# Attention, gated feed-forward and token mixing: the probabilities' fp16 parts taken straight from the exponentials, and the last attention unit's scores taken from fp32 products

## The chip, the cores and the metric

The program runs on one core of a Trainium2 chip. The engines are TensorE (PE, whose weight loads are listed apart as PEld), VectorE (DVE), ScalarE (ACT), GpSimd (POOL) and SyncE (SP), which issues every DMA here. The metric is the device time of one execution in microseconds, as the median of several runs.

## The reference

Three layers follow one another. Only the first is touched by the change.

```python
# B, H, S, D = 2, 8, 768, 64; n_sink 4, window 128
scores = (1 / sqrt(D)) * q @ k.T
keep = (key < n_sink) | ((0 <= query - key) & (query - key < window))
a = softmax(where(keep, scores, -1e9))      # row sum plus 1e-9
x = (a @ v) as (B, S, 512)

h = relu(x @ w_in)                          # 512 -> 1024
x = (h * sigmoid(conv3(h))) @ w_out         # back to 512; conv3 along the sequence

theta = x @ w_theta
y = w_tok_r @ (x * cos(theta)) + w_tok_i @ (x * sin(theta))
u = x + y
out = u + relu(u @ w_ch)
```

Everything is fp32. The weights arrive as 64-bit words and are decoded on the chip by ACT and DVE.

## The kernel before

**Products in parts.** Most products are made of three matmuls on a high part (fp32r) and a low part (the rest) of each side: `hi*hi + hi*lo + lo*hi`. The high part is a copy by ACT, the low part a subtraction by DVE. `split`, `decode` and `mm3` are the helpers.

**Attention** runs in four units of eight heads: batch 0 first half of the queries (unit 0), batch 0 second half (unit 1), then batch 1 likewise (units 2 and 3). A unit is four pairs of heads. Because of the window, a tile of 128 queries needs only its own block of keys, the block before, and the four sink keys: 260 columns, except the very first tile of a sequence, which needs 128. `head` does one head:

1. `scores`: one product for each of three query tiles. In units 0 to 2 it is one fp32 matmul against a buffer `qk` that holds both heads of a pair (L299). In unit 3 it is a "stack": `load_stack` loads q and k of one head twice, one copy below the other, ACT and DVE make fp32r parts of them (L82, L283 on ACT, L84, L284 on DVE), and two fp32r matmuls give the product (L296). The first stack head is prepared ahead, after unit 2's last pair; the schedule puts that at about 98 us.
2. DVE adds the mask and takes the row maximum (L315); ACT takes the exponential with the row sum (L319); DVE makes the reciprocal `ri` (L322, L323).
3. For 28 of the 32 heads (`NORM` is `ACT`) the probabilities then go to fp16 parts: ACT multiplies the three tiles by `ri` in place (L335), ACT casts to the high part `hi` (L345), DVE subtracts to the low part `lo` (L346), and POOL makes the parts of the sink columns (L349, L350). All lie in a buffer `pb`. SP transposes it by DMA into `pt` (L353). In the four heads of unit 0's first two pairs PE does the transpose instead.
4. `pair_out` multiplies `pt` by the values (L411), and ACT and DVE write the parts of the next layer's input `xg` (L431, L432).

A head of a first half (units 0 and 2) casts in two pieces, 128 and 512 columns; a head of a second half (units 1 and 3) in one of 768.

**The second layer** is interleaved: `Group.blocks` does a block of two 128-wide slices of the hidden layer for 256 tokens (24 matmuls into `ps_h`, 12 into `ps_x`, and ACT and DVE work between them: `h`, `cv`, `ghi`, `glo`). `BLOCKS` puts blocks behind pairs of heads, and `CHUNKS` puts the decoding of its weights behind pairs of units 0 and 1. A block needs `xg` of its tokens, hence the attention before it. The rest of the second layer and the third layer follow after unit 3.

**The order** on each engine is fixed when the program is built: a list scheduler with its own model of time places the instructions of all these loops, so a shorter step moves others. Each engine then runs its list in order. PSUM has two buffers for scores, `e` three, `pb` three, `pt` four.

Of the kernel before, what the change touches and what calls it, by code (L numbers as in the profile page):

```python
# [263 lines left out]
def stack_buffer(pool, n):  # L264
    return [pool.tile([P, w], F32R, name=f"stack{n}{i}") for i, w in enumerate((3 * P, 4 * KW, 4 * KW))]


def load_stack(tc, c, n):


    nc = tc.nc
    unit, h = divmod(n, H)
    b, half = divmod(unit, 2)
    k0, nk = (0, 3 * KW - NS) if half == 0 else (2 * KW, 4 * KW - NS)
    raw = c.stack_raw[n % 2]
    q, k1, k2 = c.stack[n % 2]
    rows = slice(h * D, (h + 1) * D)
    qr, kr = raw[:, : 3 * P], raw[:, 3 * P : 3 * P + nk]
# [712 lines left out]
```

## Time and profile before

| | |
|---|---|
| Runs | 475.7, 479.04, 496.11 us; median 479.04 |
| Profiled execution | 475.81 us, of which the span is 474.0 us |
| Unit 1 (last exponentials of units 0 and 1) | about 51 to 109 us |
| Unit 2, unit 3 | about 109 to 155 us, 155 to 203 us |
| Rest of the second layer on PE | to about 296 us |
| Third layer | to the end, 474 us |

The windows below are cut at the ends of the units. "Busy" counts the union of an engine's instructions; an instruction's duration overlaps the start of the next, so the price of one in a row of them is read from start to start. The granted clock is a share of TensorE's 2.4 GHz; its two levels are 1.2 and 2.4 GHz, so 0.93 means that about 14% of the time was at the lower one.

### The profile page before, as it was taken

The page shows a single profiled execution, that of the slowest core. Times are in us where ns is not written, and L with a number is a line of the kernel's source. Part 1 is how long each engine was busy: PE and PEld are TensorE (multiplying, and loading weights), DVE is VectorE, ACT ScalarE, POOL GpSimd, SP SyncE. Part 2 cuts the span into 40 slices and gives each one's busy share as a digit, 9 for nine tenths or more (in the row PEclk, how much of TensorE's full clock was granted, in tenths as well). Part 3 has the DMA queues.
Part 4 walks back from the last instruction along what each step waited for, and adds up shares of the span by engine and source line. Part 5 has one row for each costly group of instructions (what it writes and reads, how often), then busy time and mean ns, then how long its engine had stood idle before and what let it go on. Part 6 is the DMA issues. An engine that isn't in the chain of part 4 may idle for free.

```text
span 474.0 us, 7252 instructions
## 1 busy us (share of the span) xinstructions
PE 418.8 (88%) x2376; PEld 341.0 (72%) x2376; DVE 337.1 (71%) x870; ACT 316.2 (67%) x773; POOL 23.2 (5%) x92
## 2 busy tenths in 40 slices
PE   2877648797699899799999999899889999999994
PEld 1665336685488778688898888588668888888873
DVE  5689979997578997875699877897389973211132
ACT  2999869999999999985686877966475431100010
POOL 4101001010100101100000000000000000000000
PEclk9997778899979989899999999999989999999998
DMA  4888998567984665360434100131016730000012
GB/s 109 250 198 201 281 256 206 130 168 143 189 145 86 148 139 113 73 99 12 152 114 121 60 0 1 45 90 44 0 51 197 232 100 22 24 22 24 22 44 75
DMA packets 74589, 51.94 MB, mean 110 GB/s; under 512 B 59696, under 2 KB 63280, under 8 KB 74544
## 3 DMA queue, kind: packets, MB, share of 16 engines
q1 hardware_dynamic: 74544, 51.40, 43.6%
q8 instruction: 21, 0.34, 0.3%
q14 instruction: 24, 0.20, 0.1%
HBM read 33.95 MB, written 3.15 MB: 78 GB/s over the span
## 4 chain that ended last, share of the span: by engine, by line
PE 61%; ACT 15%; DVE 10%; DMA 9%; issue 3%; SPq 1%; POOL 0%; DVEq 0%; ACTq 0%
PE ps_y L125 7%; PE ps_y L124 7%; PE ps_y L126 7%; DMA pt<-pb 5%; PE ps_x L651 4%; PE ps_m L126 4%; PE ps_m L125 4%; PE ps_m L124 4%; PE ps_x L652 4%; PE ps_x L657 3%; PE ps_h L124 3%; PE ps_h L126 3%; PE ps_h L125 3%; ACT e L335 3%; ACT e L319 3%
## 5 line engine op out<-in xcount | busy, mean ns | idle before, releaser
L299 PE MATMUL ps_s<-qk 128*128 128x260 f32 (+1 forms) x144 | 48.7, 450 | 19.8 <-POOL sink_rows L221 8.7
L124 PE MATMUL ps_h<-xg_hi,win_hi 128*128 128x258 f32 x192 | 58.5, 306 | 1.8 <-ACT h L632 1.8
L124 PE MATMUL ps_y<-z_hi,wt_hi 128*128 128x512 f32 x144 | 57.6, 400 | 1.3 <-ACT z_hi L82 0.9
L125 PE MATMUL ps_y<-z_hi,wt_lo 128*128 128x512 f32 x144 | 57.0, 397 | 0.1
L126 PE MATMUL ps_y<-z_lo,wt_hi 128*128 128x512 f32 x144 | 56.4, 396 | 0.0
L125 PE MATMUL ps_h<-xg_hi,win_lo 128*128 128x258 f32 x192 | 55.9, 292 | 0.0
L126 PE MATMUL ps_h<-xg_lo,win_hi 128*128 128x258 f32 x192 | 55.7, 296 | 0.0
L82 ACT ACTIVATE xt_hi<-ps_t 128x512 fp32r<-128x512 f32 x24 | 13.9, 595 | 61.4 <-PE ps_t L685 61.4
L315 DVE CUSTOM_DVE_ANT_0 e<-ps_s,m 128x260 f32<-128x260 f32 (+1 forms) x96 | 37.6, 400 | 17.6 <-PE ps_s L299 12.1
L636 DVE SCALAR_TENSOR_TENSOR cv<-h,cw_t,cv 128x256 f32<-128x256 f32 x96 | 44.5, 480 | 7.4 <-ACT cv L634 6.8
L319 ACT ACTIVATE e<-e,mx 128x260 f32<-128x260 f32 (+1 forms) x96 | 47.7, 501 | 1.0 <-DVE mx L315 1.0
L299 PEld LDWEIGHTS ps_s<-qk 128*128 128x128 f32 x144 | 27.3, 226 | 28.9 <-DVE mx L315 12.0
L651 PE MATMUL ps_x<-wout_hi,ghi 128*128 128x512 f32 x96 | 41.3, 430 | 2.5 <-ACT ghi L82 2.5
L124 PEld LDWEIGHTS ps_h<-xg_hi,win_hi 128*128 128x128 f32 x192 | 38.2, 199 | 4.7 <-ACT h L632 2.6
L652 PE MATMUL ps_x<-wout_lo,ghi 128*128 128x512 f32 x96 | 40.1, 417 | 0.0
L753 DVE SCALAR_TENSOR_TENSOR slot<-ps_m,slot 128x512 f32<-128x512 f32 x12 | 8.3, 691 | 44.2 <-PE ps_m L126 44.2
L125 PEld LDWEIGHTS ps_h<-xg_hi,win_lo 128*128 128x128 f32 x192 | 38.2, 199 | 1.3
L126 PEld LDWEIGHTS ps_h<-xg_lo,win_hi 128*128 128x128 f32 x192 | 37.6, 198 | 0.9
L411 PE MATMUL ps_o<-pt,vp 128*64 128x256 f16 (+2 forms) x348 | 25.4, 268 | 13.7 <-DMA pt<-pb 11.7
L335 ACT ACTIVATE e<-e,ri 128x260 f32<-128x260 f32 (+1 forms) x84 | 36.1, 508 | 0.0
L411 PEld LDWEIGHTS <-vp 128*64 128x64 f16 (+1 forms) x348 | 18.8, 116 | 23.5 <-issue 14.9
L124 PEld LDWEIGHTS ps_y<-z_hi,wt_hi 128*128 128x128 f32 x144 | 27.1, 188 | 8.0 <-ACT z_hi L82 1.2
(146 smaller groups left out, 984.6 us busy)
## 6 DMA issues: line engine op xcount, KB each, us to landing
raw<-in_w_tok_r_dram SPq DMA_DIRECT2D x12, 384.0 KB, 3.2
raw<-in_w_tok_i_dram SPq DMA_DIRECT2D x12, 384.0 KB, 3.2
...
```

The lines of the kernel that those rows point to most:

```text
L124: nc.tensor.matmul(out, whi, xhi, start=first, stop=False)
L125: nc.tensor.matmul(out, wlo, xhi, start=False, stop=False)
L126: nc.tensor.matmul(out, whi, xlo, start=False, stop=last)
L299: nc.tensor.matmul(ps[:, :n], qk[0][:, a, i * P : (i + 1) * P], qk[1][:, o : o + n], start=True, stop=True)
L315: nc.vector.tensor_tensor_reduce(out=e[:, i, :n], in0=ps[:, :n], in1=m, scale=-1.0 / math.sqrt(D), scalar=3.0e38, op0=ALU.add, op1=ALU.min ...
L319: nc.scalar.activation(e[:, i, :n], e[:, i, :n], AF.Exp, bias=mx[:, i : i + 1], scale=-1.0, accum_out=sm[:, i : i + 1])
L335: nc.scalar.activation(e[:, i, :n], e[:, i, :n], AF.Copy, scale=ri[:, i : i + 1])
L411: nc.tensor.matmul(po[a * D : (a + 1) * D, q], w[:, a * D : (a + 1) * D], pts[a][: w.shape[0], b0:b1, :], start=(n == 0), stop=(n == len(j ...
L636: nc.vector.scalar_tensor_tensor(cv[:, n, :], h[:, n, k : GT + k], w[:, k : k + 1], cv[:, n, :], ALU.mult, ALU.add)
L651: nc.tensor.matmul(self.px[t], ghi[:, n, s], whi, start=f2 == 0 and n == 0, stop=False)
L652: nc.tensor.matmul(self.px[t], ghi[:, n, s], wlo, start=False, stop=False)
L657: nc.tensor.matmul(self.px[t], glo[:, n, s], whi, start=False, stop=f2 == FB // 2 - 1 and n == 1)
```

## The change

The in-place normalisation is gone. `hi` is now written by ACT from the exponentials with `ri` as scale, once per query tile (three instructions per head), and `lo` by DVE with one `scalar_tensor_tensor` per tile, `e*ri - hi`. POOL makes the normalised sink columns `sk` itself, a third small instruction per head. Unit 3 takes its scores as units 0 to 2 do: `load_stack`, its buffers and its parts are gone, `load_qk` serves all 16 pairs in three rotating buffers, and each tile's score is one fp32 matmul instead of two fp32r ones. The pools that were opened and closed for the stack are gone.

```diff
@@ load_qk @@
-    q, k, _ = c.qk[n % 3 if n < 2 * CC else n % 2]
+    q, k = c.qk[n % 3]
@@ load_stack: removed @@
-    for a in range(2):
-        nc.sync.dma_start(qr[a * D : (a + 1) * D], c.q[b, rows, half * 3 * P : (half + 1) * 3 * P])
-        nc.sync.dma_start(kr[a * D : (a + 1) * D], c.k[b, rows, k0 : k0 + nk])
-    split(nc, k1[:, :nk], k2[:, :nk], kr)
-    nc.scalar.activation(q, qr, AF.Copy)
-    nc.vector.tensor_tensor(q[D:], qr[D:], q[D:].bitcast(F32), ALU.subtract)
@@ scores @@
-    if len(qk) == 3:
-        n = 2 * P + NS
-        for k in qk[1:]:
-            nc.tensor.matmul(ps[:, :n], qk[0][:, i * P : (i + 1) * P], k[:, o : o + n], start=k is qk[1], stop=k is qk[2])
-        return ps
@@ head @@
+    sk = c.st.tile([P, 3, NS], F32, name="sk")[:, s0:, :]
+    nc.gpsimd.tensor_tensor(sk, e[:, s0:, P:KW], ri[:, s0:].unsqueeze(2).to_broadcast([P, ns, NS]), ALU.mult)
     for i in range(3):
-        n = P if half == 0 and i == 0 else 2 * P + NS
-        nc.scalar.activation(e[:, i, :n], e[:, i, :n], AF.Copy, scale=ri[:, i : i + 1])
-    sk = e[:, s0:, P:KW]
-    for i0, i1 in [(0, 3)] if half else [(0, 1), (1, 3)]:
...
-        nc.scalar.activation(hi, src, AF.Copy)
-        nc.vector.tensor_tensor(lo, src, hi, ALU.subtract)
+        first = half == 0 and i == 0
+        d0, d1 = (0, 1) if first else (2 * i - (1 - half), 2 * i + 1 + half)
+        src = e[:, i, :P].unsqueeze(1) if first else two_blocks(e, i, 1)[:, 0]
+        hi, lo, r = pr[:, d0:d1, :], pr[:, nb + d0 : nb + d1, :], ri[:, i : i + 1]
+        nc.scalar.activation(hi, src, AF.Copy, scale=r)
+        nc.vector.scalar_tensor_tensor(lo, src, r, hi, ALU.mult, ALU.subtract)
@@ Unit.pair @@
-            if stack:
-                while len(c.stacked) <= min(2 * n + a + 1, 8 * CC - 1):
-                    c.stacked.append(load_stack(tc, c, len(c.stacked)))
-                qk = c.stacked[2 * n + a]
```

On ACT, at a head of unit 1, the order before (names: `e` exponentials, `ri` reciprocals, `pb` the fp16 parts, `sm` row sums, `mx` row maxima, `dec_t` a weight being decoded, `xg_hi` a part of the next layer's input, `h` a block's hidden slice) is:

```order
L335 ACTIVATE e<-e,ri 128x260 x3
L100 ACTIVATE dec_t<-slot_114 128x512
L431 ACTIVATE xg_hi<-ps_o,vst 128x129
L345 ACTIVATE pb_204<-e 128x768
L319 ACTIVATE e,sm<-e,mx 128x260
L632 ACTIVATE h<-ps_h 128x258
```

And now (L310 is the scaled high part, L288 the exponential, L98 and L80 decoding and parts, L396 the next layer's input):

```order
L310 ACTIVATE pb_199<-e,ri 128x256 x3
L396 ACTIVATE xg_hi<-ps_o,vst 128x257
L98 ACTIVATE dec_t<-slot_119 128x512
L80 ACTIVATE wout_hi<-slot_114 128x512
L288 ACTIVATE e,sm<-e,mx 128x260 x2
L80 ACTIVATE ghi<-cv 128x512
```

The three scaled activations stand where the normalisation stood, write `pb` themselves, and the cast at the end of the head is gone.

On DVE, in unit 1, the low part before (L315 mask and maximum, L346 low part, L101 to L103 decoding):

```order
L101 TENSOR_SCALAR slot_115<-slot_115 128x512
L315 ISA e,mx<-ps_s,m_110 128x260
L315 ISA mx 128x1
L346 TENSOR_TENSOR pb_202<-e,pb_202 128x768
L103 SCALAR_TENSOR_TENSOR slot_119<-slot_119 128x512
L323 RECIPROCAL ri<-sm 128x3
```

And now (L311 is the low part, L284 mask and maximum, L99 to L101 decoding):

```order
L311 SCALAR_TENSOR_TENSOR pb_201<-e,ri,pb_201 128x256 x2
L284 ISA e,mx<-ps_s,m_110 128x260
L284 ISA mx 128x1
L311 SCALAR_TENSOR_TENSOR pb_201<-e,ri,pb_201 128x256
L101 SCALAR_TENSOR_TENSOR slot_118<-slot_118 128x512
L101 SCALAR_TENSOR_TENSOR slot_119<-slot_119 128x512
```

One subtraction over a head became three instructions, which the order splits around other work.

On PE, at the start of unit 3, before (L296 the two matmuls of a stack, L124 to L126 a block's first product, L411 a pair's output):

```order
L411 LDWEIGHTS vp
L411 MATMUL ps_o<-pt,vp 64x256
L126 MATMUL ps_h<-xg_lo,win_hi 128x258
L296 MATMUL ps_s<-stack_1224,stack_1223 128x260
L296 MATMUL ps_s<-stack_1225,stack_1223 128x260
L124 MATMUL ps_h<-xg_hi,win_hi 128x258
L125 MATMUL ps_h<-xg_hi,win_lo 128x258
```

And now (L268 the fp32 score, L122 to L124 the block's first product, L376 the output):

```order
L124 MATMUL ps_h<-xg_lo,win_hi 128x258
L122 MATMUL ps_h<-xg_hi,win_hi 128x258
L123 MATMUL ps_h<-xg_hi,win_lo 128x258
L268 MATMUL ps_s<-qk_120 128x260
L376 LDWEIGHTS vp
L376 MATMUL ps_o<-pt,vp 64x256
```

One fp32 score stands where two fp32r matmuls stood. Counted over the whole order, between the first score of unit 2 and the first score of unit 3 PE had 72 matmuls into `ps_h` and 28 into `ps_x`, and now has 60 and 16; the 12 and 12 stand behind, among unit 3's work. Up to the first score of unit 2 both orders hold the same 108 and 32.

## Rows read from the trace of the kernel before

**Rows 1.** The page: busy time, share of the span and instructions of each engine.

```profile
PE 418.8 (88%) x2376; PEld 341.0 (72%) x2376; DVE 337.1 (71%) x870; ACT 316.2 (67%) x773; POOL 23.2 (5%) x92
```

**Rows 2.** Windows by stage: length, then each engine's busy us, granted clock, DMA share, GB/s.

```profile
40.00:109.00 69.00, 52.01 (x316) 40.55 (x316) 63.72 (x180) 63.36 (x167) 6.44 (x22) 0.80 0.81 198
109.00:155.00 46.00, 38.95 (x281) 31.38 (x281) 32.32 (x121) 44.22 (x131) 4.39 (x20) 0.93 0.77 142
155.00:203.00 48.00, 42.96 (x316) 37.05 (x316) 42.79 (x124) 48.00 (x134) 4.44 (x16) 0.93 0.54 117
203.00:296.00 93.00, 93.00 (x588) 80.64 (x588) 72.20 (x146) 66.76 (x140) 0.41 (x2) 1.00 0.28 71
```

**Rows 3.** Timeline, ACT, two stretches: start us, us, what it ran.

```profile
101.09 0.90 ACT L634 ACTIVATE cv<-h,cw_t 128x256 f32<-128x256 f32 x2
101.89 0.36 ACT L431 ACTIVATE xg_hi<-ps_o,vst 128x129 fp32r<-128x129 f32 x1
...
102.64 1.31 ACT L335 ACTIVATE e<-e,ri 128x260 f32<-128x260 f32 x3
103.85 0.93 ACT L207 ACTIVATE slot<-slot,vst 128x768 f16<-128x768 f32 x1
...
105.69 0.83 ACT L345 ACTIVATE pb<-e 128x768 f16<-128x768 f32 x1
106.43 0.46 ACT L431 ACTIVATE xg_hi<-ps_o,vst 128x257 fp32r<-128x257 f32 x1
...
130.24 0.82 ACT L345 ACTIVATE pb<-e 128x512 f16<-128x512 f32 x2
130.96 1.19 ACT L335 ACTIVATE e<-e,ri 128x128 f32<-128x128 f32 x3
```

**Rows 4.** Timeline, DVE, unit 1.

```profile
103.41 0.88 DVE L636 SCALAR_TENSOR_TENSOR cv<-h,cw_t,cv 128x256 f32<-128x256 f32 x2
104.20 0.35 DVE L432 SCALAR_TENSOR_TENSOR xg_lo<-ps_o,vst,xg_hi 128x129 fp32r<-128x129 f32 x1
...
108.56 0.95 DVE L346 TENSOR_TENSOR pb<-e,pb 128x768 f16<-128x768 f32 x1
109.43 0.48 DVE L432 SCALAR_TENSOR_TENSOR xg_lo<-ps_o,vst,xg_hi 128x257 fp32r<-128x257 f32 x1
```

**Rows 5.** Timeline, ACT, unit 3: parts of one head's k and q.

```profile
188.97 0.69 ACT L82 ACTIVATE stack<-qk 128x524 fp32r<-128x524 f32 x1
...
189.91 0.43 ACT L632 ACTIVATE h<-ps_h 128x258 f32<-128x258 f32 x1
```

**Rows 6.** Timeline, DVE, the same head's parts.

```profile
191.31 0.70 DVE L84 TENSOR_TENSOR stack<-qk,stack 128x524 fp32r<-128x524 f32 x1
...
192.63 0.43 DVE L315 CUSTOM_DVE_ANT_0 e<-ps_s,m 128x260 f32<-128x260 f32 x1
```

**Rows 7.** Timeline, PE, two stretches around one score product each.

```profile
151.15 0.71 PE L299 MATMUL ps_s<-qk 128*128 128x260 f32 x2
151.50 0.47 PE L126 MATMUL ps_h<-xg_lo,win_hi 128*128 128x258 f32 x1
151.81 0.28 PE L124 MATMUL ps_h<-xg_hi,win_hi 128*128 128x258 f32 x1
...
182.47 0.40 PE L296 MATMUL ps_s<-stack,stack 128*128 128x260 f32 x2
182.71 0.28 PE L124 MATMUL ps_h<-xg_hi,win_hi 128*128 128x258 f32 x1
182.83 0.28 PE L125 MATMUL ps_h<-xg_hi,win_lo 128*128 128x258 f32 x1
```

**Rows 8.** The chain of waits, 56 to 72 us: start us, us, what.

```profile
58.43 10.08 DMA pt<-pb
```

**Rows 9.** Tile pb: instructions, duration in ns as min/median/max, first and last start.

```profile
L346 DVE TENSOR_TENSOR pb<-e,pb x40: 280/685/959, 42.5 to 209.6; 128x768 f16<-128x768 f32 x16, 128x128 f16<-128x128 f32 x12, 128x512 f16<-128x512 f32 x12
L349 POOL CAST pb<-e x28: 189/203/767, 37.1 to 206.5; 128x24 f16<-128x24 f32 x16, 128x8 f16<-128x8 f32 x12
```

More of the change, by code (lines that the diff above doesn't have):

```diff
@@ L48 @@
 FLAG = 3
-SK = 'gpsimd'
 WT = 8
-PRE_STACK = 1
 TOK_CUT = 2
@@ L246, in qk_buffer @@
     nc.gpsimd.memset(q[:D, 1, :], 0.0)
-    return q, k, qk
+    return q, k
 def load_qk(tc, c, n):
@@ L261, in load_qk @@
     return q, k
[L264 to L278, printed above, removed]
-    for a in range(2):
-        nc.sync.dma_start(qr[a * D : (a + 1) * D], c.q[b, rows, half * 3 * P : (half + 1) * 3 * P])
-        nc.sync.dma_start(kr[a * D : (a + 1) * D], c.k[b, rows, k0 : k0 + nk])
-    split(nc, k1[:, :nk], k2[:, :nk], kr)
-    nc.scalar.activation(q, qr, AF.Copy)
-    nc.vector.tensor_tensor(q[D:], qr[D:], q[D:].bitcast(F32), ALU.subtract)
-    return q, k1, k2
 def scores(tc, c, half, qk, i, a):
@@ L462, in pair @@
         n = (2 * b + half) * CC + p
-        stack = n >= 3 * CC
-        if not stack:
-            while len(c.loaded) <= (n + AHEAD if n + AHEAD < 2 * CC else min(n + 1, 3 * CC - 1)):
-                c.loaded.append(load_qk(tc, c, len(c.loaded)))
-            qk = c.loaded[n]
+        while len(c.loaded) <= min(n + AHEAD, 4 * CC - 1):
+            c.loaded.append(load_qk(tc, c, len(c.loaded)))
+        qk = c.loaded[n]
         pts = []
         for a in range(2):
-            if stack:
-                while len(c.stacked) <= min(2 * n + a + 1, 8 * CC - 1):
-                    c.stacked.append(load_stack(tc, c, len(c.stacked)))
-                qk = c.stacked[2 * n + a]
             pts.append(head(tc, c, half, a, qk, NORM[n][a]))
-            if n == 3 * CC - 1 and a == PRE_STACK:
-                c.stacked.append(load_stack(tc, c, 3 * H))
             if a == LAG - 1:
@@ L771, in body @@
     c.st = pool(right, "st", 4, "right")
-    early, turn = ExitStack(), ExitStack()
-    right.push(lambda *_: early.close())
     if general:
@@ L791, in body @@
         c.ps_o = pool(right, "ps_o", 2, "right", space=PSUM)
-        c.dec = pool(early, "dec", DEC, "right")
-        c.qk = c.qk[:1] + [qk_buffer(nc, pool(st, "qk", 1, side), n) for n, st, side in ((1, turn, "left"), (2, early, "right"))]
+        c.dec = pool(right, "dec", DEC, "right")
+        pq = pool(right, "qk", 1, "right")
+        c.qk = c.qk[:1] + [qk_buffer(nc, pq, n) for n in (1, 2)]
         c.pbuf = []
@@ L810, in body @@
         unit.start()
-        if n == 2 and not general:
-            early.close()
-            pq = pool(right, "stack0", 1, "right")
-            c.stack_raw = [pq.tile([P, 3 * P + 4 * KW], F32, name="stack_raw"), c.qk0]
-            c.stack = [stack_buffer(pq, 0)]
-            c.stacked = [None] * (3 * H)
-        if n == 3 and not general:
-            turn.close()
-            c.stack.append(stack_buffer(pool(turn, "stack1", 1, "left"), 1))
         for p in range(4):
@@ L834, in body @@
     nc.scalar.activation(c.scratch, c.last_sum, AF.Silu)
-    turn.close()
     right.close()
@@ L921, in moe_stack @@
         c.loaded = [load_qk(tc, c, 0)]
-        c.qk0 = c.qk[0][2]
         c.early = [weight_load(tc, c, n) for n in range(EARLY)]
```

11 lines of the change are left out of this document (2 added, 9 removed).

## Prediction

> **What bounds the kernel now.** I read the page first. PE is busy for 418.8 of 474 us and DVE and ACT for about 70% each [rows 1], so by the averages PE is the bound. The windows by stage say otherwise [rows 2]. From 203 to 296 us PE is busy without a gap: a microsecond of PE work there is a microsecond of time. In unit 3 (155 to 203) ACT is busy for all 48 us and PE for 43. In unit 2 ACT is busy for 44.2 of 46 us while DVE has 13.7 us to spare. In the stretch before, 40 to 109 us, ACT (63.4 of 69) and DVE (63.7) are level, so neither can be relieved alone. After 296 us the third layer is PE's and the change does not touch it. So the question is not how much ACT time the change removes but in which of the stages ACT is what ends last, and what PE, which gets the work in the end, pays.
>
> **Part 1, ACT of the probabilities.** Before, a head of a second half takes three normalisations, 102.64 to 103.85 us, 1.21 us, and one cast, 105.69 to 106.43, 0.74 us. After, three activations with a pointer scale over 256 columns. The block's scaling of 256 columns, the same form, takes 0.80 us for two [rows 3], so three take 1.20: the normalisations turn into the high parts at the same price, and the cast is the saving. For a first-half head the cast's two pieces take 0.72 us (130.24 to 130.96) [rows 3]. That is 16 x 0.74 + 12 x 0.72 = 20.5 us of ACT.
>
> **Part 2, DVE of the probabilities.** One subtraction of 768 columns takes 108.56 to 109.43, 0.87 us. Two scaled subtractions of 256 take 0.79 us [rows 4], three 1.19: 0.32 more for a second-half head, or 0.16 for each instruction more. A first-half head goes from two instructions to three, 0.16 more. Together 16 x 0.32 + 12 x 0.16 = 7.0 us more on DVE.
>
> **Part 3, the stack's parts.** ACT makes one head's two parts in 188.97 to 189.91, 0.94 us [rows 5], DVE in 191.31 to 192.63, 1.32 us [rows 6]. Eight heads: 7.5 us off ACT and 10.6 us off DVE. One of the eight lies at about 98 us, one at the end of unit 2, six in unit 3. Over the whole kernel ACT loses 28.0 us and DVE 3.6 net, but DVE's gain is in unit 3, and its loss in the units before.
>
> **Part 4, PE of unit 3's scores.** This is the part that speaks against the change. The fp32 product at 151.15 delays the matmuls behind it until 151.81, where without it one block matmul (0.12 us, from the two neighbours at 182.71 and 182.83) would have stood: 0.54 us. The stack's two matmuls take 182.47 to 182.71, 0.24 us [rows 7]. So each of the 24 products costs 0.30 us more, 7.2 us in all; the least I can read is to the very next matmul, which starts at 151.50: 0.35 against 0.24 us, 0.11 x 24 = 2.6, if that one's own delay is hidden. I take 6.0, near the upper end, because blocks surround these products in both orders. The Trainium skill (FP8 and Floating Point Precision, TensorE Precision Notes) says that true fp32 makes four passes through the array while reduced fp32 reads a truncated value; two passes more of 260 columns at 2.4 GHz are 0.22 us, an estimate of 5.2 us for the 24, which would make the sum 0.8 us better. The trace shows a product as two records, not four, and a price above that estimate.
>
> **Part 5, POOL and the DMAs.** One more POOL instruction per head of the sort that takes 0.2 us in the median and 0.77 at most [rows 9]. Three of these end before ACT's 1.2 us and DVE's last subtraction, which the transpose waits for too; I cost it at nothing while DVE ends last. The stack's 32 loads become 12 and SP has fewer issues; nothing waits for them in unit 3 now.
>
> **The sum, stage by stage.** It is made against the profiled execution, 475.8 us.
>
> *Up to 109 us.* ACT falls by 9.7 us (four heads at 0.72, eight at 0.74, one stack head). DVE gains 4 x 0.16 + 8 x 0.32 = 3.2 us and gives up 1.3 for the stack head: 65.6 of 69 us. DVE is then the only bound. Its idle time of 5.3 us holds the stall behind one transpose, a DMA of 10.1 us queued behind weight loads [rows 8], which no engine's speed changes. I take -1.0, between -4 (the idle time shrinks, since ACT feeds DVE's decoding sooner) and +2 (DVE's increase lies on the path).
>
> *Unit 2.* ACT falls from 44.2 by 8 x 0.72 and one stack head, 6.7 us, to 37.5. The order also moves 12 matmuls into `ps_h` and 12 into `ps_x` behind it; by 0.40 us for 256 columns ACT's share of these is about 2 us, so 35.5. At the same fill (44.2 of 46, 96%) the unit takes 37.0 us: -9.0. With nothing of the moved work counted it is 39.1, -7; if DMA latency shows up, -5; -11 if the fill rises.
>
> *Unit 3 and the rest to 296 us.* PE decides here: without its gaps unit 3 now holds more PE work than ACT or DVE work. Four terms. The moved matmuls: 12 x 0.12, and 12 of twice the columns at 0.24, +4.3. The fp32 products, +6.0. The gaps that go: 48.0 - 43.0, -5.0. The lower clock that goes with them: a granted 0.93 over 48 us at 90% busy costs 0.07 x 48 x 0.9, -3.0. I leave 2.0 us of new gaps, since PE runs its list in order and waits for a transpose now and then: +4.3, between -1 (fp32 at 2.6, no new gap) and +6.5 (7.2, and 3 us of gaps).
>
> *After 296 us.* 0, with 1.5 either way for a changed order of the third layer's first rotations.
>
> -1.0 - 9.0 + 4.3 = -5.7: **470 us**. So about four fifths of the 28 us taken from ACT bring nothing: the first stage has DVE beside ACT, and the last has PE.
>
> **Rivals.**
>
> *The first stage opens too.* The transposes start earlier since the cast is gone, PE has its outputs sooner, and DVE's decoding is fed without waits: -4, with unit 2 at -11 and the last stage at +1 (fp32 at 4.7, no new gap): -14, **462 us**. For it: ACT is 10.0 of 10 in long pieces there. Against: DVE at 63.7 of 69 has to fit 1.9 us more.
>
> *PE pays everything back.* Unit 2 gains 6, the fp32 products cost 7.2 and PE waits in order for another 3 us: -6 + 6.5 = about 0, **476 us**. For it: any PE time after 155 us counts whole. Against: the lower clock and the gaps of unit 3 are seen, and ACT's 11.6 us less there (8 x 0.74 and 6 x 0.94) removes their cause.
>
> *VectorE takes ACT's place, and the result is slower.* The low part now reads e and hi through DVE for three instructions a head, and POOL reads e once more. The Trainium skill (SBUF, Who interferes with whom) says that a DVE instruction with two SBUF inputs and a GpSimd instruction that reads SBUF hold off each other, whichever comes second. As a mechanism of this kernel: each of the 20 heads of units 0 to 2 loses a POOL instruction's 0.2 us on DVE, 4.0 us, with DVE's own 3.2 less 1.3, and unit 2 gains nothing, while PE's fp32 products stay unpaid by half (+2): **484 us**. It decides once DVE's spare 13.7 us in unit 2 lie where they can't be used. Against it: the 768-column subtraction never took over 959 ns, though POOL's cast beside it ranged from 189 to 767 [rows 9]: POOL gives way, not DVE.
>
> **How the numbers follow.** The forecast 470 has 0.55, the open first stage 0.24, the full payback 0.16, the slower one 0.05. The first three lie between 461 and 477; the executions shown differ among themselves by 3 us without the outlier at 496, so the range is 461 to 478. It leaves out the slower case and tails, 0.2 together. A measurement of this kernel tells about 2% from no change, 9.5 us. Faster by more than that: nearly all of the first rival and a sixth of the forecast, 0.33. Slower by over 2%: most of the slower case, 0.04. Within 2%: 0.63.
>
> **What would show it.** ACT's busy time falls by about 28 us and DVE's by about 4. In the stage up to 109 us the end of unit 1 hardly moves and DVE is above 94% of it. Unit 2 takes 35 to 40 us with ACT still above 93%. In unit 3 PE is above 95% busy at a granted clock near 1, ACT clearly below, and each score there delays its neighbours by about 0.5 us. The prediction is wrong if unit 1 ends more than 4 us earlier, if unit 2 stays above 42 us, or if PE still shows gaps of over 4 us between 145 and 285 us.

## The result, and the profile after

The changed kernel takes 463.93 us in the median of four runs (463.08 to 466.72), the kernel before 479.95 us in the median of four. The ratio is 0.9705, with a 95% interval of 0.9621 to 0.9789; it leaves out the run of before at 496.11 us, which stands 3% above the other three. The profiled execution takes 463.08 us with a span of 461.2, against 475.81 and 474.0: 12.7 us less, where 5.7 were forecast.

The page after, the line of engines that answers to [rows 1]:

```profile
PE 415.2 (90%) x2376; PEld 336.5 (73%) x2376; DVE 334.1 (72%) x898; ACT 291.9 (63%) x717; POOL 36.1 (8%) x120
```

ACT lost 24.3 us of busy time and DVE 3.0, near the forecast 28 and 4. POOL gained 12.9 us; its 28 more instructions are 9.3 of that, 0.2 us each in the median and 0.89 at most.

Windows cut at the ends of units 1, 2 and 3, at the first token-mixing matmul (`ps_y`, 294.6 us) and at 350 us; the first three answer to the first three of [rows 2]:

```profile
40.00:107.40 67.40, 52.40 (x317) 40.78 (x316) 64.59 (x194) 56.28 (x151) 10.95 (x28) 0.82 0.82 199
107.40:143.10 35.70, 30.41 (x245) 24.66 (x245) 28.43 (x120) 33.33 (x105) 7.48 (x24) 1.00 0.98 174
143.10:207.00 63.90, 62.57 (x444) 51.81 (x444) 49.77 (x152) 49.40 (x136) 8.60 (x29) 1.00 0.40 79
207.00:294.60 87.60, 85.68 (x518) 73.59 (x517) 68.03 (x136) 63.44 (x133) 0.62 (x3) 1.00 0.23 67
294.60:350.00 55.40, 53.78 (x242) 42.31 (x241) 48.57 (x93) 39.34 (x75) 0.00 (x0) 1.00 0.24 74
```

Unit 1 ends at 107.4 us (108.8 before) with DVE at 96%. Unit 2 takes 35.7 us (45.9 before), ACT at 93%. Unit 3 is PE's: 62.57 of 63.9 us at full clock, with ACT at 77%. The stretch from 155 to 203 us in [rows 2] had it the other way round, ACT full and PE at 43 of 48.

The new steps. Timeline of ACT, unit 2: three high parts (128, 256 and 256 columns), twice; the row behind gives the price from start to start, 1.09 us:

```profile
127.33 1.21 ACT L310 ACTIVATE pb<-e,ri 128x128 f16<-128x128 f32 x3
128.42 0.52 ACT L591 ACTIVATE cv<-h,cw_t 128x256 f32<-128x256 f32 x1
...
133.76 1.23 ACT L310 ACTIVATE pb<-e,ri 128x128 f16<-128x128 f32 x3
134.85 0.54 ACT L288 ACTIVATE e<-e,mx 128x260 f32<-128x260 f32 x1
```

Timeline of DVE, unit 2: low parts of 256 columns, 0.39 us (134.08 to 134.47) and 0.40 us (134.53 to 134.93), the price taken from [rows 4]:

```profile
134.08 0.47 DVE L311 SCALAR_TENSOR_TENSOR pb<-e,ri,pb 128x256 f16<-128x256 f32 x1
134.47 0.15 DVE L204 TENSOR_SCALAR vst<-vst 128x1 int32<-128x1 int32 x1
134.53 0.47 DVE L311 SCALAR_TENSOR_TENSOR pb<-e,ri,pb 128x256 f16<-128x256 f32 x1
134.93 0.48 DVE L397 SCALAR_TENSOR_TENSOR xg_lo<-ps_o,vst,xg_hi 128x257 fp32r<-128x257 f32 x1
```

Timeline of PE, unit 3: an fp32 product between matmuls of 512 columns, which come every 0.23 us where nothing delays them. It answers to [rows 7]:

```profile
189.67 0.60 PE L268 MATMUL ps_s<-qk 128*128 128x260 f32 x2
189.92 0.58 PE L608 MATMUL ps_x<-wout_hi,ghi 128*128 128x512 f32 x1
190.34 0.39 PE L609 MATMUL ps_x<-wout_lo,ghi 128*128 128x512 f32 x1
190.57 0.39 PE L608 MATMUL ps_x<-wout_hi,ghi 128*128 128x512 f32 x1
```

From 189.67 to 190.34 are 0.67 us; less the 0.23 of the matmul that started in between, the product costs 0.44 us, not the 0.54 that I read at 151.15. That row [rows 7] has a six-matmul group of 128 columns right ahead of it, which the prediction didn't weigh. The stack's parts [rows 5, 6] are gone.

**Where the 12.8 us of span went.** Every microsecond of the span is PE at work, PE idle, or PE at a lower granted clock (busy time times one minus the granted clock, added up over windows of 5 us). This split was missing in the prediction. Before and after, by stage:

| Stage | length | PE idle | lost to the clock |
|---|---|---|---|
| to the end of unit 1 | 108.8 -> 107.4 | 31.3 -> 30.2 | 9.7 -> 9.1 |
| unit 2 | 45.9 -> 35.7 | 7.0 -> 5.3 | 3.2 -> 0 |
| unit 3 | 48.1 -> 63.9 | 5.0 -> 1.3 | 2.4 -> 0 |
| to the first `ps_y` | 96.7 -> 87.6 | 0 -> 1.9 | 0 -> 0 |
| about 60 us from there | 60.5 -> 55.4 | 5.5 -> 1.6 | 1.6 -> 0 |
| the rest | 114.0 -> 111.2 | 6.3 -> 5.6 | 0 -> 0.2 |
| all | 474.0 -> 461.2 | 55.1 -> 45.9 | 16.8 -> 9.3 |

So 9.2 us are idle time that went, 7.5 a lower clock that went, and PE's work at full clock rose by 4.0 us (402.0 to 406.0). How the two hang together, two windows of unit 2 in the kernel before show (length, PE busy, and the granted clock after POOL's column):

```profile
125.60:131.50 5.90, 3.10 (x26) 1.98 (x22) 2.49 (x11) 5.90 (x18) 0.78 (x4) 0.80 0.64 157
131.50:137.40 5.90, 5.90 (x34) 5.57 (x34) 5.54 (x20) 5.90 (x19) 0.39 (x2) 0.62 1.11 136
```

PE stood still for 2.8 of 5.9 us, and in the stretch behind, with PE busy all along, the granted clock was 0.62: most of it ran at 1.2 GHz, the lower of the two levels, and 38% of the 5.9 us were lost. After the change no window of unit 2 is below 1.00.

### The profile page after: what moved, and what is told of

The parts are those of the page before. It is cut to its first block, busy times and chain, and to the rows that moved or that the text cites. A ratio compares the mean times of both kernels' runs of the same rounds, so it can differ in the third digit from the quotient of the medians.

```text
span 461.2 us, 7197 instructions
## 1 busy us (share of the span) xinstructions
PE 415.2 (90%) x2376; PEld 336.5 (73%) x2376; DVE 334.1 (72%) x898; ACT 291.9 (63%) x717; POOL 36.1 (8%) x120
## 4 chain that ended last, share of the span: by engine, by line
PE 63%; DVE 10%; ACT 5%; DMA 5%; issue 1%; SPq 0%; POOL 0%; ACTq 0%
PE ps_y L123 7%; PE ps_y L124 7%; PE ps_y L122 7%; PE ps_m L124 5%; PE ps_m L122 5%; PE ps_m L123 4%; PE ps_x L608 4%; PE ps_x L609 4%; PE ps_x L614 4%; DMA pt<-pb 3%; PE ps_h L122 3%; PE ps_h L124 3%; PE ps_h L123 3%; PE ps_s L268 3%; PE ps_o L376 2%; PE ps_t L642 2%
## 5 line engine op out<-in xcount | busy, mean ns | idle before, releaser
L268 PE MATMUL ps_s<-qk 128*128 128x260 f32 (+1 forms) x192 | 62.1, 436 | 13.7 <-DVE par_flag L150 8.7
L122 PE MATMUL ps_h<-xg_hi,win_hi 128*128 128x258 f32 x192 | 59.4, 310 | 1.4 <-ACT xg_hi L396 1.1
L122 PE MATMUL ps_y<-z_hi,wt_hi 128*128 128x512 f32 x144 | 57.6, 400 | 0.0
L124 PE MATMUL ps_y<-z_lo,wt_hi 128*128 128x512 f32 x144 | 56.5, 395 | 0.0
L124 PE MATMUL ps_h<-xg_lo,win_hi 128*128 128x258 f32 x192 | 55.1, 292 | 0.0
L80 ACT ACTIVATE xt_hi<-ps_t 128x512 fp32r<-128x512 f32 x24 | 14.2, 595 | 60.4 <-PE ps_t L642 60.4
L268 PEld LDWEIGHTS ps_s<-qk 128*128 128x128 f32 x192 | 35.0, 215 | 23.9 <-issue 10.8
L284 DVE CUSTOM_DVE_ANT_0 e<-ps_s,m 128x260 f32<-128x260 f32 (+1 forms) x96 | 37.7, 400 | 19.6 <-PE ps_s L268 17.3
L288 ACT ACTIVATE e<-e,mx 128x260 f32<-128x260 f32 (+1 forms) x96 | 47.0, 493 | 7.0 <-DVE mx L284 6.8
L608 PE MATMUL ps_x<-wout_hi,ghi 128*128 128x512 f32 x96 | 40.1, 418 | 0.2 <-ACT ghi L80 0.2
L122 PEld LDWEIGHTS ps_h<-xg_hi,win_hi 128*128 128x128 f32 x192 | 37.2, 194 | 4.2 <-ACT xg_hi L396 1.7
L123 PEld LDWEIGHTS ps_h<-xg_hi,win_lo 128*128 128x128 f32 x192 | 37.2, 194 | 2.3 <-DVE win_lo L82 0.6
L609 PE MATMUL ps_x<-wout_lo,ghi 128*128 128x512 f32 x96 | 38.0, 396 | 0.0
L124 PEld LDWEIGHTS ps_h<-xg_lo,win_hi 128*128 128x128 f32 x192 | 36.8, 194 | 1.2
L376 PE MATMUL ps_o<-pt,vp 128*64 128x256 f16 (+2 forms) x348 | 24.7, 259 | 13.1 <-DMA pt<-pb 9.4
L311 DVE SCALAR_TENSOR_TENSOR pb<-e,ri,pb 128x256 f16<-128x256 f32 (+1 forms) x84 | 35.3, 459 | 1.4 <-ACT pb L310 1.4
L310 ACT ACTIVATE pb<-e,ri 128x256 f16<-128x256 f32 (+1 forms) x84 | 35.4, 491 | 1.3 <-DVE ri L292 0.7
L376 PEld LDWEIGHTS <-vp 128*64 128x64 f16 (+1 forms) x348 | 18.1, 112 | 24.2 <-issue 19.6
```

The costliest lines, as they stand in the source:

```text
L122: nc.tensor.matmul(out, whi, xhi, start=first, stop=False)
L123: nc.tensor.matmul(out, wlo, xhi, start=False, stop=False)
L124: nc.tensor.matmul(out, whi, xlo, start=False, stop=last)
L268: nc.tensor.matmul(ps[:, :n], qk[0][:, a, i * P : (i + 1) * P], qk[1][:, o : o + n], start=True, stop=True)
L284: nc.vector.tensor_tensor_reduce(out=e[:, i, :n], in0=ps[:, :n], in1=m, scale=-1.0 / math.sqrt(D), scalar=3.0e38, op0=ALU.add, op1=ALU.min ...
L288: nc.scalar.activation(e[:, i, :n], e[:, i, :n], AF.Exp, bias=mx[:, i : i + 1], scale=-1.0, accum_out=sm[:, i : i + 1])
```

## The experiments

Ratios are to the kernel before, with 95% intervals. "Idle" and "clock" are the columns of the table above. Ends of units are the ends of their last exponentials.

| Kernel | median us | ratio | unit 1 ends | unit 2 takes | idle | clock |
|---|---|---|---|---|---|---|
| changed kernel | 463.93 | 0.9705 (0.9621 to 0.9789) | 107.4 | 35.7 | 45.9 | 9.3 |
| e1 probabilities only | 464.03 | 0.9696 (0.9666 to 0.9727) | 111.8 | 35.9 | 54.2 | 8.9 |
| e2 scores only | 479.06 | 1.0006 (0.9973 to 1.0038) | 110.6 | 51.3 | 54.8 | 14.4 |
| e3 before, sixth rotation early | 475.63 | 0.9935 (0.9904 to 0.9965) | 109.7 | 46.8 | 55.1 | 19.6 |
| e4 changed, sixth rotation late | 469.53 | 0.9822 (0.9778 to 0.9865) | 108.9 | 36.8 | 48.8 | 10.8 |
| e5 e1, sixth rotation early | 465.42 | 0.9695 (0.9666 to 0.9724) | 111.3 | 36.1 | 50.4 | 11.2 |
| e6 fp32 products twice | 473.95 | 0.9867 (0.9838 to 0.9895) | 109.1 | 36.7 | 45.8 | 11.5 |
| e7 low parts on POOL | 462.68 | 0.9642 (0.9611 to 0.9672) | 106.7 | 36.3 | 45.9 | 8.8 |
| e8 old form in units 0, 1 | 471.33 | 0.9805 (0.9774 to 0.9836) | 110.5 | 40.7 | 52.2 | 13.6 |
| e9 no low parts | 460.41 | 0.962 (0.9576 to 0.9663) | 107.1 | 34.3 | 43.5 | 10.5 |
| e10 no scale of sums | 461.67 | 0.9666 (0.963 to 0.9701) | 105.6 | 40.4 | 44.5 | 8.5 |
| e11 sink product five times | 465.7 | 0.9725 (0.9678 to 0.9773) | 108.1 | 35.5 | 45.0 | 11.7 |
| e12 half the loads | 463.51 | 0.968 (0.9635 to 0.9725) | 97.4 | 40.7 | 46.6 | 7.1 |

Kernels with the same order of PE up to there differ by up to 1.7 us in the end of unit 1 (changed, e4, e6 and e11: 107.4 to 109.1; before and e3: 108.8 and 109.7), and the clock's column by 2.8 us; smaller differences say nothing. The changed kernel's interval is wide, since it rests on three runs of the kernel before: those of all kernels but e2, e3 and e6 overlap it. e4 and e8 do so by 0.0011 and 0.0015 only, and none of their runs (467.13 us and more) is as short as the longest of the changed kernel (466.72).

### e1 and e2: the two halves of the change

e1 takes `head` from the changed kernel and everything else from the kernel before; e2 the reverse. The piece that they exchange:

```diff
-        nc.scalar.activation(e[:, i, :n], e[:, i, :n], AF.Copy, scale=ri[:, i : i + 1])
...
-        nc.scalar.activation(hi, src, AF.Copy)
-        nc.vector.tensor_tensor(lo, src, hi, ALU.subtract)
+        nc.scalar.activation(hi, src, AF.Copy, scale=r)
+        nc.vector.scalar_tensor_tensor(lo, src, r, hi, ALU.mult, ALU.subtract)
```

e1:

> The kernel before with the probabilities' half of the change alone; unit 3 keeps its stacked parts of q and k. Theory: ACT's relief counts in unit 2, and the rest of the gain is idle time and lower clock on PE from 143 us on; the fp32 products only cost (about 4 us of PE work at full clock, from 402 to 406 us). Then this kernel has the gain of unit 2 (8 to 9 us, one stack head of ACT still in it), PE work of about 402 us, and 464 to 470 us in all; in its order the sixth rotation comes after the last ps_x matmul, which the theory charges with 3 to 5 us. Rival: the stack's parts on DVE (10.6 us) and ACT (7.5) keep unit 3 bound, so that dropping them is needed: 473 to 477.

e2:

> The changed kernel with the old normalisation, cast and subtraction; unit 3 takes its scores from fp32 products. Theory: unit 2 stays bound by ACT (44 to 46 us, less about 1 for the one stack head), PE work rises by 4 us, ACT in unit 3 falls by 6 x 0.94 us and opens part of its 5 us of gaps: 474 to 480, no change. Rival: the scores' half carries the gain through unit 3 and what follows: 466 to 470.

e1 measured 464.03: the whole gain, and the rival (473 to 477) is out. Unit 2 gains its 10 us with one stack head still in it. e2 measured 479.06 with an interval around 1: the scores' half by itself is worth nothing. Its unit 2 took 51.3 us, not the 44 to 46 expected; its order has 83 matmuls into `ps_h` and 40 into `ps_x` there, the kernel before 72 and 28. Added to e1 it is worth nothing either: it raises PE's work and takes about as much idle time away (54.2 to 45.9 us).

### e3, e4 and e5: the third layer's order

The table `ROTATE` says how many rotations of batch 0 are emitted behind each of the last eight blocks. In the changed kernel the scheduler put the products of all six rotations (72 matmuls of `ps_m`) ahead of the last `ps_x` matmul, in the kernel before only those of five (60). e3 makes the kernel before do the first:

```diff
-ROTATE = (1, 2, 0, 0, 0, 1, 0, 2)
+ROTATE = (1, 2, 0, 0, 0, 1, 1, 1)
```

> The kernel before with one number of the table of rotations moved, so that the sixth rotation's product stands before the last ps_x matmul, as in the changed kernel; attention is the same word for word. Theory: the 7.9 us that the changed kernel gains after the first token-mixing matmul are an effect of the order alone: fewer PE gaps and no lower clock from 297 to 360 us, 470 to 473 in all (4 to 5 us of gaps and clock; the rest is work that only changes sides). Rival: those gaps went since DVE and ACT come out of attention with less behind them; then this order brings nothing: 475 to 478.

e4 makes the changed kernel do the second:

```diff
-ROTATE = (1, 2, 0, 0, 0, 1, 0, 2)
+ROTATE = (1, 2, 0, 0, 0, 0, 1, 2)
```

> The changed kernel with one number of the table of rotations moved, so that the sixth rotation's product stands behind the last ps_x matmul, as in the kernel before. Theory (the order): it gives back 3 to 5 us, 467 to 469, with new PE gaps between 290 and 360 us. Rival (less behind DVE and ACT): 463 to 465, no new gaps.

Windows of about 60 us from the first `ps_y` matmul, PE's busy time and granted clock. The kernel before:

```profile
299.50:360.00 60.50, 54.96 (x238) 42.58 (x237) 48.34 (x89) 39.72 (x74) 0.00 (x0) 0.97 0.18 56
```

e3, the same attention, sixth rotation early; its first `ps_y` starts at 307.0 us, and the first of the two rows is the stretch from the end of unit 3 up to there:

```profile
204.60:307.00 102.40, 98.28 (x613) 84.27 (x611) 76.66 (x151) 73.43 (x153) 0.41 (x2) 1.00 0.27 65
307.00:367.00 60.00, 58.48 (x260) 46.35 (x261) 52.38 (x102) 40.68 (x77) 0.00 (x0) 1.00 0.26 85
```

e4, the changed attention, sixth rotation late:

```profile
296.00:356.00 60.00, 54.46 (x237) 42.56 (x237) 47.80 (x91) 38.36 (x71) 0.00 (x0) 0.97 0.23 69
```

With the late order PE has 5.5 us of gaps in either kernel and a granted clock of 0.97; with the early one the clock is 1.00, and the gaps are 1.5 us in e3 and 1.6 in the changed kernel (its last window above). But the early order opens gaps just ahead of this mark: between the end of unit 3 and the first `ps_y` matmul PE is idle for 4.1 us in e3 and 1.9 in the changed kernel, and not at all in the kernel before and in e4. So the order is best priced from the place where PE's orders part to the end. There e3 takes 192.2 us (from 281.0 on) and the kernel before 194.9 (from 279.1 on), 2.7 less; the changed kernel takes 198.4 us (from 262.8 on) and e4 202.5 (from 264.3 on), 4.1 less.

By the medians, e3 gains 0.65%, 3.1 us of the 478.57 that the kernel before took beside it. That is less than the theory's 4 to 5, and its 475.63 us lie in the rival's range, but the interval excludes the rival's nothing. e4 is 5.6 us above the changed kernel, more than the theory gave, and has the gaps that the rival excludes; 1.5 us of its span were lost before the orders part, with the same instructions. So the order by itself is worth about 3 to 4 us, with attention unchanged.

e5 adds the early order to e1:

> The kernel before with the probabilities' half alone, and the sixth rotation's product before the last ps_x matmul (one number of the table moved). Theory: the two gains add, the unit-2 gain with its PE idle time, and 3 to 5 us of PE gaps that the order left after 292 us: 459 to 462, below the changed kernel, since the fp32 products are not paid. Rival: with no stacked parts dropped, DVE and ACT are behind after attention whatever the order: 463 to 465.

It brought nothing (ratio 0.9695 after 0.9696). e1 has neither of the two orders: there the scheduler had put twelve `ps_y` matmuls ahead of the sixth rotation, so its gap was filled. With the edit e1's third layer has fewer gaps in its first 60 us (1.1 for 4.3 us), but 3.2 instead of 0.6 ahead of it, and 1.2 us of lower clock. The two gains don't add.

### e6: the price of the fp32 products

```diff
-ROTATE = (1, 2, 0, 0, 0, 1, 0, 2)
+ROTATE = (1, 2, 0, 0, 0, 1, 1, 1)
...
-    nc.tensor.matmul(ps[:, :n], qk[0][:, a, i * P : (i + 1) * P], qk[1][:, o : o + n], start=True, stop=True)
+    c.nsc = getattr(c, "nsc", 0) + 1
+    for _ in range(2 if c.nsc > 72 else 1):
+        nc.tensor.matmul(ps[:, :n], qk[0][:, a, i * P : (i + 1) * P], qk[1][:, o : o + n], start=True, stop=True)
```

> The changed kernel with each of unit 3's 24 score products issued twice into the same bank, the second over the first; the table of rotations is set so that the third layer keeps the changed kernel's order. With PE 98% busy there, the difference is the price of 24 fp32 products. The prediction's reading (0.54 us each, 0.30 above the two reduced ones): +13, 475 to 479. Its lower end (0.35 each): +8.4, 471 to 473. The four-pass estimate (0.46 each): +11, 474 to 475. Rival (PE has slack in unit 3 and the products fall into it): +0 to +4.

The span is 10.9 us longer than the changed kernel's (472.1 to 461.2), but 1.5 of these are there before PE's orders part (at 143.0 and 141.5 us). The 9.4 left are 0.39 us for each of the 24, and the median, 473.95, lies between the expectations of the lower end and of the four passes. Timeline of PE in e6, one doubled and one single product, with block matmuls (one every 0.12 us) behind each:

```profile
189.48 1.04 PE L270 MATMUL ps_s<-qk 128*128 128x260 f32 x4
190.17 0.48 PE L122 MATMUL ps_h<-xg_hi,win_hi 128*128 128x258 f32 x1
190.48 0.28 PE L123 MATMUL ps_h<-xg_hi,win_lo 128*128 128x258 f32 x1
...
195.35 0.60 PE L270 MATMUL ps_s<-qk 128*128 128x260 f32 x2
195.60 0.47 PE L122 MATMUL ps_h<-xg_hi,win_hi 128*128 128x258 f32 x1
195.91 0.28 PE L123 MATMUL ps_h<-xg_hi,win_lo 128*128 128x258 f32 x1
```

Two products: 189.48 to 190.48, less 0.12, 0.88 us. One: 195.35 to 195.91, less 0.12, 0.44 us. So the fp32 form costs 0.44 - 0.24 = 0.20 us more than two reduced ones, 4.8 us for the change, where the prediction had 6.0; the 4.0 us more of PE's work at full clock agree. So do the other single products of unit 3 that stand right before a block matmul: 0.47 us in the mean of eleven in the changed kernel, 0.28 for eleven stacks in the kernel before. The Trainium skill (FP8 and Floating Point Precision, TensorE Precision Notes) gives true fp32 four passes through the array. The trace agrees: four times 260 columns at 2.4 GHz are 0.433 us, beside the measured 0.44. Of the two readings that the prediction set side by side, the page's was the better.

### e7, e9 and e11: is DVE the bound up to 107 us, and what does POOL do to it

e7 gives one instruction of the weights' decoding to POOL:

```diff
-        nc.vector.tensor_tensor(lo, src, hi.bitcast(F32), ALU.subtract)
+        (sub or nc.vector).tensor_tensor(lo, src, hi.bitcast(F32), ALU.subtract)
...
-                decode_parts(nc, c.dec, raw, hi[:, r % 2, :], lo[:, r % 2, :], INPLACE)
+                decode_parts(nc, c.dec, raw, hi[:, r % 2, :], lo[:, r % 2, :], INPLACE, sub=nc.gpsimd)
```

> The changed kernel with the expert weights' low parts (16 subtractions of 512 columns, all up to 107 us) made by POOL instead of DVE. Theory: DVE ends last up to 107 us, so 16 x 0.6 = 9.6 us less on it end unit 1 by 3 to 8 us earlier, and about half of that is left at the end: 459 to 462. Rival 1: the late transposes and ACT's chain set that stage, the end of unit 1 moves by less than 1.5 us: 463 to 465. Rival 2 (VectorE and GpSimd hold each other off): DVE's instructions beside POOL's take longer, unit 1 ends later: 466 or more.

Unit 1 ended at 106.7 us, 0.7 earlier, as the first rival has it, and the ratio's interval overlaps the changed kernel's. Groups of DVE's instructions up to the end of unit 1 (busy us, mean ns of one), the changed kernel:

```profile
L311 DVE SCALAR_TENSOR_TENSOR pb<-e,ri,pb 128x256 f16<-128x256 f32 x26 | 11.7, 478 | 0.0
L101 DVE SCALAR_TENSOR_TENSOR slot<-slot 128x512 int32<-128x512 int32 x16 | 11.0, 690 | 0.0
L593 DVE SCALAR_TENSOR_TENSOR cv<-h,cw_t,cv 128x256 f32<-128x256 f32 x16 | 7.6, 478 | 0.0
```

The same in e7:

```profile
L311 DVE SCALAR_TENSOR_TENSOR pb<-e,ri,pb 128x256 f16<-128x256 f32 x26 | 14.8, 592 | 0.0
L101 DVE SCALAR_TENSOR_TENSOR slot<-slot 128x512 int32<-128x512 int32 x16 | 12.7, 795 | 0.0
L593 DVE SCALAR_TENSOR_TENSOR cv<-h,cw_t,cv 128x256 f32<-128x256 f32 x14 | 8.3, 620 | 0.0
```

Each kind takes 15 to 30% longer. DVE gave away 16 subtractions, 10.7 us of busy time, and was as busy all the same: 92.5 us up to the end of unit 1, against 93.0. One place shows it. Timeline of POOL in e7:

```profile
73.30 1.29 POOL L82 TENSOR_TENSOR win_lo<-slot,win_hi 128x512 fp32r<-128x512 f32 x1 [1.54 <-ACT win_hi L80]
```

Timeline of DVE in e7, same place:

```profile
73.33 1.54 DVE L311 SCALAR_TENSOR_TENSOR pb<-e,ri,pb 128x256 f16<-128x256 f32 x1
```

DVE's subtraction was issued 0.03 us behind POOL's and ended 0.28 us after it: by these times it stood still for nearly all of POOL's. Two more scaled subtractions of 256 columns began while a long one of POOL's ran; they took 1.52 us each and also ended 0.28 us after it. The 46 that met no POOL instruction took 0.47 to 0.48. The Trainium skill (SBUF, Who interferes with whom) says that a DVE instruction with two SBUF inputs and a GpSimd instruction that reads SBUF exclude each other for the whole instruction, the later one waiting. e7 agrees. This is the mechanism of the prediction's slower rival, and e7 tells its price when POOL's instruction is long (1.29 us).

e11 asks for the short ones:

```diff
-    nc.gpsimd.tensor_tensor(sk, e[:, s0:, P:KW], ri[:, s0:].unsqueeze(2).to_broadcast([P, ns, NS]), ALU.mult)
+    for _ in range(5):
+        nc.gpsimd.tensor_tensor(sk, e[:, s0:, P:KW], ri[:, s0:].unsqueeze(2).to_broadcast([P, ns, NS]), ALU.mult)
```

> The changed kernel with POOL's added product of the sink columns made five times over (same result, PE's order the same word for word): 28 x 4 = 112 more POOL instructions of 12 columns at most that read the exponentials, some 23 us of POOL. Theory: so short a POOL instruction costs DVE nothing that can be seen, only long ones do (e7): the scaled subtractions keep 0.48 us, 463 to 466. Rival (each POOL instruction that reads SBUF holds DVE off for its length): 112 x 0.2 = 22 us more DVE time, of which the 10 up to 107 us and some in unit 2 count: 472 to 480. Rival 2 (the transpose waits for POOL's chain, 0.8 us longer a head): 466 to 469 by waits of PE for the transposed probabilities.

It measured 465.7, a ratio whose interval holds the changed kernel's. POOL's busy time doubled, from 36.1 to 70.5 us:

```profile
PE 418.5 (90%) x2376; PEld 339.6 (73%) x2376; DVE 334.4 (72%) x898; ACT 292.4 (63%) x717; POOL 70.5 (15%) x232
```

and DVE's scaled subtractions up to 107 us were no longer than before:

```profile
L312 DVE SCALAR_TENSOR_TENSOR pb<-e,ri,pb 128x256 f16<-128x256 f32 x26 | 11.6, 473 | 0.0
```

Over the whole of e11, 35 scaled subtractions of 256 columns began while one of POOL's short instructions was running, and took 0.45 to 0.49 us. The rule just cited makes no exception for short instructions; for these the measurement decides, and the runs don't show why. So the cost of "nothing" for POOL's added instruction held, and the slower rival had no ground in this change.

e9 relieves DVE without POOL:

```diff
-        w1 = [part_tiles(c, "win") for _ in range(CC // 2)]
+        w1 = [part_tiles(c, "win")[:1] * 2 for _ in range(CC // 2)]
...
-                decode_parts(nc, c.dec, raw, hi[:, r % 2, :], lo[:, r % 2, :], INPLACE)
+                t = c.dec.tile([P, DM], F32, name="dec_t")
+                nc.scalar.activation(tiles[r // 2][0][:, r % 2, :], decode(nc, raw, t, INPLACE), AF.Copy)
```

> The changed kernel without the 16 subtractions of 512 columns that make the low parts of the expert weights (left out: these low parts; their matmuls take the high parts instead, as many and of the same shape). DVE is relieved as in e7, by 10.7 us up to 107 us, but POOL gets nothing. Theory: DVE ends last in that stage, and e7 gained nothing there since POOL's long subtractions lengthened DVE's own instructions; now the scaled subtractions of 256 columns stay at 0.48 us (0.59 in e7), unit 1 ends at 99 to 104 us, and the whole takes 458 to 463 (its third layer has the late order, 3 to 5 us). Rival: the late transposes and ACT set that stage; unit 1 ends at 106 to 109 us, 466 to 469.

DVE's instructions in e9 up to the end of unit 1:

```profile
L284 DVE CUSTOM_DVE_ANT_0 e<-ps_s,m 128x260 f32<-128x260 f32 x40 | 16.8, 422 | 11.5 <-PE ps_s L268 11.2
L311 DVE SCALAR_TENSOR_TENSOR pb<-e,ri,pb 128x256 f16<-128x256 f32 x29 | 13.0, 473 | 0.0
L101 DVE SCALAR_TENSOR_TENSOR slot<-slot 128x512 int32<-128x512 int32 x16 | 11.0, 688 | 0.0
```

They kept their length (473 ns, not 592), so POOL was e7's trouble. But unit 1 ended at 107.1 us: the rival. DVE had 10.7 us less to do and waited 11.2 us for scores instead (3.7 in the changed kernel). **DVE was not the only bound of that stage.** Waits between 45 and 107 us in e9 (total, times, longest, in us) point at another:

```profile
PE ps_o L376 <- DMA pt<-pb: 11.5, 3, 5.8
DVE e L284 <- PE ps_s L268: 7.3, 4, 5.2
PE ps_o L231 <- DMA vp<-slot: 1.8, 1, 1.8
```

The first and the last are DMA transposes, of the probabilities and of the values: 13.3 us, where the changed kernel has 3.8 and 5.1. The median of the whole was 3.5 us lower nevertheless, though its order is the late one: PE's idle time fell to 43.5 us. The intervals overlap, so this gain is not shown.

### e12: the loads

```diff
-                raw, slot = c.wraw.pop(0) if c.wraw else weight_load(tc, c, c.nw)
-                c.nw += 1
+                if r % 2 == 0:
+                    raw, slot = c.wraw.pop(0) if c.wraw else weight_load(tc, c, c.nw)
+                    c.nw += 1
```

> e9 with half of the expert weights' loads as well (left out, beside the low parts: 8 of the 16 loads of 512 KB; a loaded block is decoded twice in their place, with the same instructions on every engine). In e9 unit 1 ended at 107.1 us although DVE had 10.7 us less to do, and PE waited 13.3 us between 45 and 107 us for transposes that landed late, while the DMA engines were above full share from 40 to 70 us. Theory: the weight loads in the queues hold the transposes up, and PE, which runs its list in order, waits: with half the loads those waits fall below 6 us, unit 1 ends at 97 to 103 us, and the whole takes 450 to 457. Rival: the chain of one head after another through ACT and DVE sets that stage whatever the loads; unit 1 ends at 105 to 108 us, 458 to 462.

Unit 1 ended at 97.4 us, 9.7 earlier than in e9, and PE's waits for transposes up to there fell from 13.3 to 6.5 us:

```profile
PE ps_o L376 <- DMA pt<-pb: 4.2, 3, 2.9
PE ps_o L231 <- DMA vp<-slot: 2.3, 1, 2.3
```

So with DVE relieved, half of the loads less ends the stage far earlier than equal orders differ by, and the rival is out. That this comes of the transposes queued behind the loads is not shown: from 40 us to the end of unit 1 the transposes of `pb` took 4.3 us in the median in e9 and 4.4 in e12 (9.5 and 6.6 at most), ACT's 2.4 us of waits for weights went as well, and the two kernels differ in PE's order from 16 us on. Of the 9.7 us, split as in the table above, 2.9 are idle time of PE and 7.7 a lower clock that went, less 0.9 by which its work came out longer. Whether fewer loads alone would do it, with DVE at 96%, was not tried. The time of the whole was missed: 463.51 us, not 450 to 457. Units 2 and 3 in e12:

```profile
97.40:138.10 40.70, 32.60 (x240) 26.92 (x236) 29.56 (x121) 34.47 (x105) 6.54 (x25) 0.96 0.81 142
138.10:200.00 61.90, 61.66 (x437) 50.95 (x436) 49.14 (x152) 49.24 (x135) 8.57 (x26) 1.00 0.43 84
```

and in e9:

```profile
107.10:141.40 34.30, 32.08 (x241) 25.48 (x237) 29.41 (x118) 32.50 (x103) 7.77 (x26) 1.00 0.88 179
141.40:196.00 54.60, 54.60 (x388) 45.93 (x386) 44.21 (x144) 44.56 (x130) 9.39 (x24) 1.00 0.49 86
```

102.6 us against 88.9, so the lead was gone by the end of unit 3: PE had 8.1 us of gaps in unit 2 (2.2 in e9), and unit 3, where PE is full in both, held 7.1 us more of its work. PE's idle time was 46.6 us in all, no less than in the changed kernel.

### e8: the old form in the first two units

```diff
+    if c.npb <= 12:
+        for i in range(3):
+            n = P if half == 0 and i == 0 else 2 * P + NS
+            nc.scalar.activation(e[:, i, :n], e[:, i, :n], AF.Copy, scale=ri[:, i : i + 1])
...
+            nc.scalar.activation(hi, src, AF.Copy)
+            nc.vector.tensor_tensor(lo, src, hi, ALU.subtract)
+    else:
...
```

> The changed kernel with the old normalisation, cast and one subtraction in units 0 and 1, and the new form in units 2 and 3. Theory: up to 107 us DVE ends last, so 8.6 us more on ACT and 3.2 less on DVE leave the end of unit 1 within 1.5 us: 463 to 466. Rival (the first stage opens by ACT's relief): unit 1 ends 3 us later or more, 467 to 469.

It measured 471.33, above both expectations. Unit 1 ended 3.1 us later than in the changed kernel, as the rival has it (up to 1.7 us of this is within what equal orders differ by), and unit 2 took 5.0 us longer although its heads are in the new form. Waits of PE in unit 2 for transposed probabilities, e8:

```profile
PE ps_o L392 <- DMA pt<-pb: 7.6, 3, 3.8
```

and the changed kernel:

```profile
PE ps_o L376 <- DMA pt<-pb: 4.2, 4, 2.4
```

e8's order has 36 matmuls into `ps_h` among the scores of unit 2 where the changed kernel has 60, so PE has less to do while transposes are under way. Whether ACT's 8.6 us or only the new order costs the 7 us (5 by the ratios) stays open, since every edit of `head` gives a new order.

### e10: a smaller version

```diff
-    nc.vector.tensor_scalar(sm, sm, 1.0e-9, 1.0 / SP, ALU.add, ALU.mult)
...
-    nc.vector.tensor_scalar(unscale.bitcast(I32), bits, 1.0, -float(26 << 23), ALU.mult, ALU.add)
+    nc.vector.tensor_scalar(unscale.bitcast(I32), bits, 1.0, -float(14 << 23), ALU.mult, ALU.add)
```

> The changed kernel without the small DVE instruction that adds 1e-9 to the sums and scales them (the sum holds exp(0) = 1, so the addition changes nothing in fp32; the factor of 4096 goes, and the values' unscaling with it). 15 x 0.16 = 2.4 us less on DVE up to 107 us, and 0.16 us less from each head's exponentials to its transpose. Theory: unit 1 ends 1 to 3 us earlier, the whole takes 460 to 463 if the new order costs nothing. Rival: DVE's 0.16 us lie in idle time, 463 to 465.

461.67 us, and unit 1 ends 1.8 us earlier: inside the theory's range. But the interval of its ratio overlaps the changed kernel's, and so do those of e1 and e7: none of these is told from the changed kernel.

## Why the prediction was right in its range, and where it was off

*Up to 109 us: -1.0 forecast, -1.4 measured.* The end hardly moved, as forecast, and the 1.4 us are no more than equal orders differ by. The reason did not hold: "DVE is then the only bound" was wrong, since e9 took 10.7 us from DVE and the end stayed. The weight loads, behind which the same paragraph sees a transpose queued [rows 8], bound the stage too: it ended earlier once half of them were gone as well (e12).

*Unit 2: -9.0 forecast, -10.2 measured.* Right, with its mechanism: ACT filled 96% of it, e1 shows the gain without the scores' half, and ACT filled 93% of it afterwards. By the table above, 5.3 of the 10.2 us are PE work that now stands behind the unit, as the moved matmuls of the forecast have it; e10, with the same heads but 84 matmuls into `ps_h` and 38 into `ps_x` up to the first score of unit 3, takes 40.4 us there, not 35.7. The forecast left out that the unit's lower clock went with the gaps, 3.2 us.

*Unit 3 and the rest: +4.3 forecast, +6.7 measured to the first `ps_y` matmul.* In these 6.7 lie eight transposes by PE (`ps_t`) that the new order brings ahead of that mark, 8 x 0.11 = 0.9 us, and the 1.9 us of gaps that the early order opens there (e3 has such gaps, e4 and the kernel before have none); like for like it is +3.9. The fp32 term was too high (4.8 for 6.0, e6), the gaps that went were 3.7 net in unit 3, and the lower clock gave back 2.4 (3.0 forecast).

*After 296 us: "0, with 1.5 either way for a changed order of the third layer's first rotations".* **This is the term that was mis-sized.** From the first `ps_y` matmul on, the changed kernel takes 166.6 us, the kernel before 174.5: -7.9. Of these, 0.9 are the transposes done earlier and 1.9 are paid by the new gaps just ahead, so -5.1 is real: 2.7 us of gaps (3.9 + 0.7 less the 1.9), 1.4 of lower clock (1.6 less 0.2 later), and 1.0 by which the other work came out shorter. e3 and e4 show that the order alone is worth 2.7 us in one kernel and 4.1 in the other; what the rest comes from is not shown. The prediction had named the mechanism and priced it at no more than 1.5, without a view of the stretch behind [rows 2]: there, from 299.5 to 360 us, the window of the kernel before has 5.5 us of gaps and a granted clock of 0.97, so that much was to be won or lost by an order.

*The rivals.* The measured time is within 2 us of the first rival's 462, but not by its mechanism: the first stage did not open (-1.4, not -4). That the range held the result is in part luck: it reached so low for the sake of this rival, and the time got there mostly by the third layer. Nor is the rival's mechanism out altogether: e8 leaves open how much of ACT's relief the end of the first stage needed. PE did not pay everything back. VectorE did not take ACT's place in this change; e7 shows what it would have taken.

*The sum.* -1.4 - 10.2 + 3.9 - 5.1 = -12.8 for -5.7. Of the 7 us between, 5.1 are the third layer's, 1.2 unit 2's, 0.4 each the other two.
